# Top-k attention and two MLPs on one core: the first batch's values loaded once, and another drawn order of all instructions

## The chip, the cores and the metric

The program runs on one core of a Trainium2 chip, as one launch. The metric is the device time of a run in microseconds, taken as the median of several runs. The core's engines are TensorE (PE, with its weight loads as PEld), VectorE (DVE), ScalarE (ACT), GpSimd (POOL) and SyncE (SP); here SP issues every DMA, and its queue is served in order.

## The reference

For 4 batches of 8 heads, 576 positions and 64 channels:

```python
scores = scale * np.matmul(q, k.transpose(0, 1, 3, 2))
kth = np.partition(scores, -32, axis=-1)[..., -32:-31]
scores = np.where(scores >= kth, scores, -1e9)
attn = softmax(scores)                # max subtracted, sum + 1e-9
x = np.matmul(attn, v)                # -> 2304 tokens x 512
x = softplus(x @ w_in1) @ w_out1      # 512 -> 2048 -> 512
h = x @ w_in2
x = (h - tanh(h)) @ w_out2
```

All arrays are float32. The kernel keeps each operand as a sum of two float16 numbers (hi and lo), scaled by a power of two, and forms three products of every matrix product.

## The kernel before, in words

**Work.** The 576 queries of a batch are four tiles of 128 and a rest of 64. A chunk is two tiles of one batch (256 tokens); the rests of two batches form a chunk of their own. A visit (`visit_load`, L1205) is one pair of heads of one chunk; there are 32. It loads keys, queries and values of the pair, and the second visit to a pair takes the prepared keys and values back from a copy in DRAM. Per tile of a visit: scores on PE (`front`), copied to SBUF by ACT, four MAX8 and three MATCH_REPLACE8 on DVE to find the 32nd largest, an exponential on ACT, the hi and lo halves on ACT and POOL, a DMA transpose (pT), the product with the values on PE (`back`, L1400), and at the end of a visit a transpose into the chunk's x (tiles xy).

**Weights.** Each of the four weight matrices comes in 8 groups of 1 MB (`weight_load`, L867). A group is cast on ACT, combined on DVE, squared and summed on PE for its scale (`weight_convert`, L918), and split into whi and wlo (`weight_split`, L962): whi on ACT for all four; wlo on POOL for the first and the fourth, on PE and ACT for the second, on DVE for the third. While a tile is not yet needed, its room serves as staging: parts of whi and wlo of the later matrices hold raw weights or constants.

**MLP.** Once a chunk's x is complete, each layer runs in 8 steps: `gemm1` (24 matmuls into h), an activation on ACT (and DVE and POOL), `gemm2` into y. Layer 1 of a chunk needs all of the first two matrices; layer 2 the last two.

**Scales of the values.** Before the values of a batch can be split (`visit_prep_v`, L1302: one ACT and one DVE instruction of 128x640 per pair), a power-of-two scale is needed. `v_norm` (L1039) loads all values of the batch a second time, as five pieces of 128x460 into free xy tiles, squares each on ACT with a running sum, and forms the scale `sx` on DVE and PE. For batch 0 that is called where the loop over tiles stands at n == VN, which is 0. The pair's own values come by three DMAs in `visit_load`, into a single buffer v (NVR = 1), so that the next pair's load waits for the split of the one ahead.

**Order.** All operations are first recorded (`Recorder`), each with a rank from its place in the program. `order` (L557) lays them out with a list scheduler (`place`) that has a cost for every instruction: the ranks get random noise from SEED, the schedule is refined over TURNS rounds, and the best is taken. Then each entry of SHIFTS moves the ranks again: one with a number draws noise of a given size for the operations of some engines in a time window, one with names (V: values, P: preparation of a visit, N: norms, L and W: load and conversion of weights, M: MLP, S: tiles) adds a constant. The result is a fixed order on every engine. `idle` (L594) puts filler matmuls, whose result nobody reads, into longer gaps that the plan foresees on PE (L664).

Already in the file stands `first_v_load` (L1189), which with V0 = 1 takes the place of `v_norm(0)` and of the value loads of batch 0's visits; with V0 = 0 it isn't called.

Of the kernel before, what the change touches and what calls it, by code (L numbers as in the profile page):

```python
# [44 lines left out]
V0 = 0  # L45
# [33 lines left out]
SEED = 1322  # L79
# [12 lines left out]
VN = 0  # L92
# [7 lines left out]
NH = 2  # L100
NPX = 2
# [21 lines left out]
QLM = 0  # L123
SPC = 640.0

SHIFTS = (
# [12 lines left out]
    (22991, 679021, 687021, 2500, "PDAGS"), ("M0", 220737, 520737, -300, "PDAG"), (72979, 149882, 157882, 200, "PDAGS"),  # L139
# [3 lines left out]
    (86590, 883276, 903276, 2500, "SA"), (94052, 867481, 875481, 1000, "PDAGS"), (39752, 741704, 801704, 200, "PDAGS"),  # L143
# [10 lines left out]
    (63116, 1018776, 1168776, 1000, "PDAGS"), ("N2", 277145, 317145, -3000, "PDAGS"), (79700, 731025, 751025, 200, "PDAGS"),  # L154
# [7 lines left out]
    (275, 843642, 863642, 2500, "PDAGS"), (54408, 328307, 336307, 200, "PDAGS"), ("P", 183450, 191450, -10000, "PDAGS"),  # L162
# [9 lines left out]
    ("S,P,V", 81321, 101321, -1000, "PDAG"), (32745, 441991, 741991, 100, "S"), (6720, 146714, 166714, 400, "PDAGS"),  # L172
# [498 lines left out]
def topk_attention_two_mlps(  # L671
# [64 lines left out]
    def spare(early=None):  # L736
# [3 lines left out]
        if not early:  # L740
            return al("px", NPX, [P, 512], F32, pb)
# [831 lines left out]
    def new_acc(T):  # L1573
        return [al("y", 2, [P, 512], F32, pb) for _ in range(T // P)]
# [353 lines left out]
```

## Time and profile before

| | |
|---|---|
| median of 3 runs | 1112.79 us (1110.7 to 1116.18) |
| the profiled execution: time, span | 1111.59 us, 1109.9 us |
| granted TensorE clock, mean | 0.977 |
| busy over the span: PE, DVE, ACT, POOL | 998.6, 928.0, 898.2, 769.7 us |
| weight loads on PE (PEld) | 785.7 us |
| data moved by DMA | 152.06 MB, of it 73.01 MB read from HBM |
| PE in the chain that ended last | 58% (DVE 15%, ACT 10%, POOL 7%) |

The table is one execution on the chip. Busy shares over the whole span hide that the stages differ: in forty equal slices of the span PE stands at 2 to 7 tenths in the first six and at 9 or more nearly everywhere after; DVE stands at 9 or 10 tenths from the second to the thirty-third slice and near zero at the end; the DMA engines are full in the first five. So the stages are read one at a time.

### The profile page before, as it was taken

How to read it: one execution, taken by the hardware profiler on the slowest of the kernel's cores; microseconds unless marked ns; L12 is line 12 of the kernel's file. 1: busy time of each engine (PE TensorE's matmuls, PEld its weight loads, DVE VectorE, ACT ScalarE, POOL GpSimd, SP SyncE). 2: the span in 40 equal slices, each digit the busy share in tenths (PEclk: the TensorE clock that was granted, in tenths of full speed). 3: DMA queues.
4: the chain of work that ended last, by engine and by line, in shares of the span. 5: the costliest groups of instructions: out<-in, count | busy, mean ns of one | idle time of the engine just before them, and what ended most of it. 6: DMA issues, size and time to landing. Idle time of an engine off the chain costs nothing.

```text
span 1109.9 us, 27484 instructions
## 1 busy us (share of the span) xinstructions
PE 998.6 (90%) x9996; PEld 785.7 (71%) x9996; DVE 928.0 (84%) x2059; ACT 898.2 (81%) x1825; POOL 769.7 (69%) x1136
## 2 busy tenths in 40 slices
PE   2446749989889999999999999999999999999998
PEld 1323437867578767876899778876787689967965
DVE  3999999989999999799999999999999999310111
ACT  6999999989899988788999898988888777643422
POOL 6795438998888666568987675787957667443423
PEclk9999868999999999999999999999999999999999
DMA  9999996538777856437877565566755462300000
GB/s 289 279 284 273 292 283 182 150 91 184 138 166 190 213 95 132 69 71 150 187 156 168 114 144 108 76 139 130 148 108 101 88 126 46 49 6 20 2 10 20
DMA packets 317496, 152.06 MB, mean 137 GB/s; under 512 B 264624, under 2 KB 308656, under 8 KB 317360
## 3 DMA queue, kind: packets, MB, share of 16 engines
q1 hardware_dynamic: 317360, 150.30, 60.3%
q8 instruction: 78, 1.28, 0.5%
q14 instruction: 58, 0.48, 0.1%
HBM read 73.01 MB, written 15.37 MB: 80 GB/s over the span
## 4 chain that ended last, share of the span: by engine, by line
PE 58%; DVE 15%; ACT 10%; POOL 7%; issue 5%; DMA 4%; SPq 0%; ACTq 0%; POOLq 0%; DVEq 0%
PE h L667 26%; PE y L667 24%; DVE m L667 6%; DVE x L667 5%; PE px L667 4%; PE s L667 4%; ACT ssb L667 2%; ACT x L667 2%; POOL hl L667 2%; POOL wlo L667 1%; ACT wlo L667 1%; ACT whi L667 1%; DMA pT<-hl 1%; ACT hl L667 1%; ACT r L667 1%
## 5 line engine op out<-in xcount | busy, mean ns | idle before, releaser
L667 PEld LDWEIGHTS <-whi 128*128 128x128 f16 (+1 forms) x3994 | 373.1, 99 | 85.7 <-DVE whi L667 25.7
L667 PE MATMUL h<-xy,whi 128*128 128x256 f16 (+1 forms) x2560 | 395.3, 262 | 2.2 <-DVE xy L667 1.9
L667 PE MATMUL h<-xy,wlo 128*128 128x256 f16 (+1 forms) x1280 | 324.7, 262 | 0.0
L667 DVE MAX8 m<-x 128x8 f32<-128x576 f32 x432 | 313.7, 745 | 0.7
L667 POOL TENSOR_TENSOR hl<-x,hl 128x512 f16<-128x512 f32 (+1 forms) x288 | 217.3, 771 | 77.5 <-ACT hl L667 63.5
L667 PEld LDWEIGHTS <-wlo 128*128 128x128 f16 (+1 forms) x1986 | 195.4, 99 | 39.1 <-DVE wlo L667 11.8
L667 DVE MATCH_REPLACE8 x<-m,x 128x576 f32<-128x576 f32 x288 | 212.7, 740 | 0.0
L667 PE MATMUL y<-g,whi 128*128 128x256 f16 (+1 forms) x1280 | 200.5, 263 | 1.2 <-POOL g L667 1.2
L667 PE MATMUL y<-whi,g 128*128 128x512 f16 x576 | 194.4, 379 | 3.0 <-POOL g L667 3.0
L667 POOL TENSOR_TENSOR g<-r,g 128x512 f16<-128x512 f32 (+1 forms) x160 | 171.9, 1076 | 15.9 <-PE y L667 8.4
L667 PE MATMUL y<-g,wlo 128*128 128x256 f16 (+1 forms) x640 | 163.1, 263 | 0.0
L667 DVE SCALAR_TENSOR_TENSOR r<-h,hinb,r 128x512 f32<-128x512 f32 (+1 forms) x80 | 54.9, 688 | 116.7 <-ACT r L667 116.4
L667 PEld LDWEIGHTS <-g 128*128 128x128 f16 x864 | 81.2, 98 | 75.9 <-POOL g L667 3.9
L667 ACT ACTIVATE x<-ssb,nb,tiny 128x576 f32<-128x576 f32 x136 | 117.6, 866 | 10.2 <-DVE m L667 5.5
L667 PE MATMUL s<-kT,qT 128*128 128x288 f16 x512 | 91.2, 304 | 29.2 <-ACT ssb L667 14.9
L667 DVE MAX8 m<-ssb 128x8 f32<-128x576 f32 x144 | 107.3, 745 | 10.7 <-ACT ssb L667 10.0
L667 PEld LDWEIGHTS <-pT 128*128 128x128 f16 (+1 forms) x2240 | 89.7, 102 | 32.1 <-issue 16.5
L667 PE MATMUL y<-wlo,g 128*128 128x512 f16 x288 | 109.1, 379 | 0.0
L667 DVE MATCH_REPLACE8 x<-m,ssb 128x576 f32<-128x576 f32 x144 | 106.5, 739 | 0.0
L667 PE MATMUL px<-vhl,pT 128*128 128x65 f16 (+1 forms) x2240 | 96.1, 196 | 8.9 <-DMA pT<-hl 5.3
L667 POOL TENSOR_SCALAR r<-r,gsb 128x512 f32<-128x512 f32 (+1 forms) x80 | 52.6, 658 | 66.3 <-ACT g L667 65.8
L667 ACT CAST hl<-x 128x576 f16<-128x576 f32 x144 | 96.1, 670 | 0.5
(153 smaller groups left out, 1616.2 us busy)
## 6 DMA issues: line engine op xcount, KB each, us to landing
whi<-in_moe_w_in_dram SPq DMA_DIRECT2D x11, 1023.0 KB, 7.5
whi<-in_moe_w_out_dram SPq DMA_DIRECT2D x7, 1023.5 KB, 6.4
vd<-vhl SPq DMA_DIRECT2D x16, 330.0 KB, 4.3
vhl<-vd SPq DMA_DIRECT2D x16, 330.0 KB, 3.4
kd<-kT SPq DMA_DIRECT2D x32, 160.0 KB, 2.8
kT<-kd SPq DMA_DIRECT2D x32, 160.0 KB, 2.7
xy<-in_moe_w_out_dram SPq DMA_DIRECT2D x18, 255.8 KB, 3.0
qraw<-in_q_dram SPq DMA_DIRECT2D x32, 128.0 KB, 3.4
```

What stands on the lines that cost most here:

```text
L667: fn(*a, **k)
```

## The change

Four things. V0 = 1 and VN = 1: for batch 0 the values are loaded once by `first_v_load`, four pairs with three DMAs each, at the next loop position; pair 0 into the buffer v, pairs 1 to 3 into a part of wlo of the third matrix that is not yet written; four ACT squares of 128x640 give the scale. The place of pairs 1 to 3 in that tile is turned round, so that pair 3 lies highest. A new SEED and a new list of SHIFTS draw another order of everything. And three lines about PSUM buffers (NYB, pw, y3) are added, whose conditions need NPX == 1; NPX is 2 here.

```diff
-V0 = 0
+V0 = 1
-SEED = 1322
+SEED = 1962
-VN = 0
+VN = 1
+NYB = 2
...
 SHIFTS = (
-    (14983, 315778, 335778, 1000, "A"), (37653, 130389, 150389, 6000, "G"),
...
+    (86327, 773281, 1073281, 100, "G"), ("N2", 206017, 2000000, 1000, "PDAGS"),
...
         if not early:
-            return al("px", NPX, [P, 512], F32, pb)
+            one = NPX == 1 and "y3" not in slots
+            return al("pw" if one else "px", 1 if one else NPX, [P, 512], F32, pb)
         turn_[0] += 1
-        return al("hy"[turn_[0] % 2], 2, [P, 512], F32, pb)
+        return al("hy"[turn_[0] % 2], (NH, NYB)[turn_[0] % 2], [P, 512], F32, pb)
...
-                c = (NG - 1) * GW - 2 * 2 * (NB + 1) * D * p
+                c = (NG - 1) * GW - 2 * 2 * (NB + 1) * D * (NP - p)
...
     def new_acc(T):
-        return [al("y", 2, [P, 512], F32, pb) for _ in range(T // P)]
+        if NPX == 1 and wdone[0] == 4 * NG and "y3" not in slots:
+            slots["y3"] = [0, slots["y"][1] + slots["pw"][1]]
+        tag, n = ("y3", 3) if "y3" in slots else ("y", 2)
+        return [al(tag, n, [P, 512], F32, pb) for _ in range(T // P)]
```

`first_v_load`, which was in the file and is now called:

```python
def first_v_load():
    ss = al("vss", 2, [P, NP], F32, cap=5)
    for p in range(NP):
        dst = first_v[p]
        nc.sync.dma_start(dst[:, :, 0:NB, :], v[0, 2*p : 2*p+2, 0 : NB*P, :]...)
        for r in (slice(0, SL), slice(SL, P)):
            nc.sync.dma_start(dst[r, :, NB, :], v[0, 2*p : 2*p+2, NB*P : S, :]...)
        j, st = xy_take([P, 2 * (NB + 1) * D], F16, "vst")
        xy_free.append(j)
        nc.scalar.activation(st, dst..., AF.Square, accum_out=ss[:, p : p + 1])
    tot = tiny()
    nc.vector.tensor_reduce(tot, ss, axis=AX.X, op=ALU.add)
    pow2_scale(col_norm(tot, 1), sx[0], ix[0])
```

## Rows read from the trace of the kernel before

**Rows 1.** Stages of the span: busy PE, PEld, DVE, ACT, POOL; clock, DMA, GB/s

```profile
0.00:172.00 172.00, 86.91 (x621) 56.49 (x622) 152.43 (x351) 156.70 (x315) 105.70 (x144) 0.88 1.05 280
172.00:260.00 88.00, 80.14 (x790) 68.03 (x789) 82.62 (x191) 82.64 (x183) 85.13 (x131) 0.96 0.58 147
260.00:480.00 220.00, 209.80 (x2109) 165.36 (x2107) 211.93 (x475) 195.34 (x409) 163.12 (x245) 0.99 0.69 146
480.00:960.00 480.00, 476.05 (x5211) 386.56 (x5209) 463.30 (x1009) 412.68 (x837) 360.83 (x547) 1.00 0.59 119
960.00:1110.00 150.00, 145.72 (x1279) 109.28 (x1275) 17.76 (x36) 50.84 (x84) 54.92 (x70) 1.00 0.05 13
```

**Rows 2.** The same view for the filler matmuls alone (L664): PE, PEld

```profile
172.00:260.00 88.00, 9.65 (x76) 7.27 (x76) 0.96 0.58 147
260.00:480.00 220.00, 4.94 (x25) 2.61 (x25) 0.99 0.69 146
480.00:960.00 480.00, 1.17 (x9) 0.89 (x9) 1.00 0.59 119
```

**Rows 3.** Timeline: last transpose into the first chunk's x, first matmul of the MLP

```profile
168.16 1.20 SPq L667 DMA_TRANSPOSE xy<-xs  x1
172.24 0.63 PE L667 MATMUL h<-xy,whi 128*128 128x256 f16 x2
```

**Rows 4.** ACT before 172 us, grouped: busy, mean ns of one | idle before

```profile
L667 ACT CAST wlo<-whi 128x1024 f16<-128x1024 bf16 x17 | 22.9, 1345 | 6.2 <-DMA whi<-in_moe_w_in_dram 6.2
L667 ACT ACTIVATE whi<-whi,tiny 128x1024 f16<-128x1024 f32 x17 | 21.0, 1236 | 1.1 <-DVE tiny L667 1.0
...
L667 ACT ACTIVATE xy<-xy 128x460 f32<-128x460 f32 x12 | 7.0, 592 | 0.0
...
L667 ACT CAST wlo<-wlo 128x1024 f16<-128x1024 bf16 x5 | 6.7, 1341 | 0.0
L667 ACT CAST wlo<-xy 128x256 f16<-128x256 bf16 x15 | 6.4, 501 | 0.0
...
L667 ACT ACTIVATE vhl<-v,tiny 128x640 f16<-128x640 f32 x4 | 3.3, 833 | 0.0
L667 ACT ACTIVATION_READ_ACCUMULATOR xy<-xy 128x1 f32 x15 | 3.0, 201 | 0.0
```

**Rows 5.** DMA engines before 172 us: packets, data, rate

```profile
DMA packets 59555, 48.09 MB, mean 280 GB/s; under 512 B 39316, under 2 KB 56724, under 8 KB 59540
```

**Rows 6.** SP's queue in order of time: issues of batch 0's values

```profile
6.15 3.00 SPq L667 DMA_DIRECT2D v<-in_v_dram  x2
...
17.33 1.69 SPq L667 DMA_DIRECT2D xy<-in_v_dram  x3
...
26.80 0.56 SPq L667 DMA_DIRECT2D xy<-in_v_dram  x1
...
48.45 0.52 SPq L667 DMA_DIRECT2D v<-in_v_dram  x1
...
93.44 1.46 SPq L667 DMA_DIRECT2D v<-in_v_dram  x2
```

**Rows 7.** The chain that ended last, two pieces of the opening: start, us

```profile
58.73 0.62 SPq L667
...
62.86 4.94 DMA kraw<-in_k_dram
```

**Rows 8.** Timeline: the scale of batch 0's values, and its first use

```profile
35.64 0.19 DVE L667 TENSOR_SCALAR tiny<-n 128x1 int32<-128x1 int32 x2
...
43.80 0.83 ACT L667 ACTIVATE vhl<-v,tiny 128x640 f16<-128x640 f32 x1
```

**Rows 9.** DVE before 172 us, grouped: one form of the top-k

```profile
L667 DVE MAX8 m<-x 128x8 f32<-128x576 f32 x57 | 41.9, 747 | 0.1
```

**Rows 10.** Timeline of DVE: batch 0's last values split, third matrix's first wlo

```profile
109.90 0.87 DVE L667 SCALAR_TENSOR_TENSOR vhl<-v,tiny,vhl 128x640 f16<-128x640 f32 x1
...
128.82 0.47 DVE L667 SCALAR_TENSOR_TENSOR wlo<-xy,tiny,whi 128x256 f16<-128x256 f32 x1
```

More of the change, by code (lines that the diff above doesn't have):

```diff
@@ L123 @@
 QLM = 0
+NYB = 2
 SPC = 640.0
 SHIFTS = (
[12 rows of a table removed]
-    (22991, 679021, 687021, 2500, "PDAGS"), ("M0", 220737, 520737, -300, "PDAG"), (72979, 149882, 157882, 200, "PDAGS"),
[3 rows of a table removed]
-    (86590, 883276, 903276, 2500, "SA"), (94052, 867481, 875481, 1000, "PDAGS"), (39752, 741704, 801704, 200, "PDAGS"),
[10 rows of a table removed]
-    (63116, 1018776, 1168776, 1000, "PDAGS"), ("N2", 277145, 317145, -3000, "PDAGS"), (79700, 731025, 751025, 200, "PDAGS"),
[7 rows of a table removed]
-    (275, 843642, 863642, 2500, "PDAGS"), (54408, 328307, 336307, 200, "PDAGS"), ("P", 183450, 191450, -10000, "PDAGS"),
[9 rows of a table removed]
-    ("S,P,V", 81321, 101321, -1000, "PDAG"), (32745, 441991, 741991, 100, "S"), (6720, 146714, 166714, 400, "PDAGS"),
[13 rows of a table removed]
[6 rows of a table added]
+    (45861, 315750, 355750, 100, "PDAGS"), (74532, 672388, 732388, 100, "D"), (40357, 597981, 657981, 100, "PDAGS"),
[9 rows of a table added]
+    (85308, 310569, 350569, 100, "PDAGS"), (41834, 1002330, 1022330, 6000, "PDAGS"), (86243, 727558, 787558, 400, "SA"),
[6 rows of a table added]
+    (18309, 200830, 220830, 200, "PDAGS"), (2026, 977709, 1277709, 6000, "PDAGS"), ("W2", 207490, 357490, 20000, "PDAGS"),
[17 rows of a table added]
+    (2993, 1004414, 1024414, 2500, "PDAGS"), (36391, 313315, 373315, 100, "D"), (50062, 298444, 306444, 1000, "PDAGS"),
[7 rows of a table added]
+    (88304, 209604, 217604, 400, "PDAGS"), (4748, 161365, 181365, 100, "PDAGS"), (39302, 102789, 122789, 2500, "PD"),
[8 rows of a table added]
+    (24339, 973107, 1013107, 6000, "PDAGS"), (4225, 572153, 632153, 2500, "S"), (46791, 593738, 613738, 200, "PDAGS"),
+    (36113, 682980, 702980, 1000, "A"), (89711, 528204, 536204, 400, "A"), (7941, 510941, 530941, 200, "A"), (55060, 744424, 764424, 6000, "S"),
+    (62163, 329902, 349902, 2500, "G"), (65759, 811680, 819680, 6000, "P"), (53464, 551140, 571140, 1000, "D"), (81936, 827662, 847662, 200, "PDAGS"),
+    (28563, 833653, 873653, 100, "PDAGS"), (44601, 753307, 761307, 1000, "A"), (93312, 882130, 890130, 400, "PDAGS"),
+    (10851, 816201, 1116201, 100, "PDAGS"), (35963, 847784, 855784, 2500, "G"), (86908, 814315, 874315, 400, "PDAGS"),
+    (75628, 671644, 691644, 400, "SA"), (44943, 777816, 785816, 2500, "PDAGS"), (13754, 182796, 202796, 100, "PDAGS"),
[6 rows of a table added]
 )
```

113 rows, old and new, of the table SHIFTS are left out of this document.

## The prediction

> **What bounds the kernel now.** I read the stages of the span first [rows 1]. From 480 us on PE is busy 476.1 of 480 us and 145.7 of 150: nothing that the change touches is short there. Before 480 us it is not so. Until 172 us PE is busy 86.9 us, while ACT is busy 156.7 and DVE 152.4 of 172 (from about 20 us on they have hardly a gap), and the DMA engines stand at a share of 1.05. From 172 to 480 us PE is busy 289.9 of 308 us, but 14.6 of that are fillers whose result nobody reads [rows 2], so useful PE work is 275.3 of 308, 89%; DVE, with 294.6 of 308, paces it. Next the timeline where the MLP begins [rows 3]: the last transpose into the first chunk's x is issued at 168.2, and the first matmul into h runs at 172.2. All later PE work is fixed by the problem, so the time is the start of the MLP, plus that work, plus the gaps behind the start. The gaps are 26.3 us idle (7.9, 10.2, 4.0 and 4.3 in the last four stages, 0.1 of it past the span's end) and 15.8 us of fillers, 42 us together. A change can win in two places: an earlier start, which ACT and DVE set, or smaller gaps before 480 us.
>
> **The change part by part.**
>
> *The three lines on PSUM buffers* ask for NPX == 1, and NPX and NH are 2: the same buffers are handed out as before. Nothing.
>
> *The squares for the scale.* Five ACT squares of 128x460 with their accumulator reads go: 5 x (0.592 + 0.201) = 3.97 us [rows 4]. Four of 128x640 come. The trace has no square of that size; the ACT instruction of that shape on the same values takes 0.833, so 4 x (0.833 + 0.201) = 4.14. Below, the 460-wide price would make it 3.2, above, scaling 0.592 by 640/460 gives 4.1. I take +0.2 us on ACT, which has no cover before 172 us.
>
> *The loads.* Five DMAs of 230 KB go (1.15 MB); the twelve loads by pair stay the same in number and bytes, and move to one block at the next loop position. Two costs hang on this. The DMA engines move 48.09 MB in the opening at 280 GB/s [rows 5], so 1.15 MB are 4.1 us of theirs; that is the gain if they set the pace, and nothing if they don't. And SP's queue loses the five norm issues of 17.3 to 26.8 us; nine value issues stood between 48.5 and 94.9 us, 6.4 us of queue time over seven rows of which the first and the last are shown [rows 6]. These stand in front of the transposes pT, kT and qT and of the key loads, on which the tiles of chunk 0 hang. What the chain shows of that is less: one value issue of 0.62 us lies on it, a few issues ahead of a key load of 4.94 us [rows 7]. So from 0.6 (the chain) to 6.4 us (all nine) can be won there if the block in front is hidden, and up to 7.4 us lost (twelve issues at 0.62) if it is not. I take -3.2 us, half of the nine issues, since the queue is loaded and the chain passes through it, but only once with a value issue on it.
>
> *The scale, one tile later.* The scale is written at 35.8 us and first used at 43.8 [rows 8], 8.0 us of slack. Moving the call by one tile is one tile of top-k, 7 x 0.747 = 5.2 us [rows 9], less than the slack. Nothing; without the cover 5.2 us.
>
> *The parking place.* Pairs 1 to 3 lie in wlo of the third matrix until their split. In the order of before the last split begins at 109.9 and ends at 110.8 us, and DVE first writes the third matrix's wlo at 128.8 [rows 10]: 18 us of cover, and pairs 1 to 3 start only in the fourth group. Nothing; if the new order drew weight groups forward by more than that, the DVE write would wait, and behind it on DVE the top-k of chunk 0. In return the single buffer v no longer makes each pair's load wait for the split ahead; no such wait of length is on the chain, so I give it nothing.
>
> *The order.* Here the trace of before has no row, only bounds. A weight group costs ACT 1.345 + 1.236 = 2.58 us [rows 4]. Before 172 us ACT casts 17 + 5 + 15/4 = 25.75 groups. The first layer of chunk 0 needs 16; 9.75 stand ahead of it that it doesn't need, and 6.25 of all 32 stand behind. Pushing all 9.75 back would start the MLP 25.2 us sooner; pulling all 6.25 ahead would start it 16.1 us later. I take the middle of the two ends, -4.5 us, something under two groups. That the sign is negative is the weakest step here.
>
> *The sum.* +0.2 - 3.2 - 4.5 = -7.5 us at the start of the MLP. Not all of it reaches the end: until 480 us PE does useful work for only 89% of the time because DVE and the others feed it, so of a sooner start that share gets through, -6.7 us; what is late next is the x of the second and third chunk, which waits for top-k on DVE. The profiled execution took 1111.6 us (span 1109.9 and 1.7 around it): 1104.9. The median of the runs is 1.2 above the profiled one, so 1106 for the median.
>
> **The rivals.** About 0.5%, 5.6 us, is what a measurement of this kernel can tell from no change.
>
> *The transfers were hidden anyway* (1112.8). The opening is paced by ACT and DVE, whose work the change doesn't lessen (+0.2 us), and the order is worth nothing on the chip. For it: ACT's and DVE's busy time in the opening, and that a single long DMA wait after the first microseconds is on the chain [rows 1, 7]. Against it: SP's part in the chain. 1112.8 + 0.2 = 1113. Beside the DMA share of 1.05 stands a rule of the Trainium skill (Perfetto Trace Analysis, Identifying the Most-Contended Engine): occupancy of the sixteen DMA engines misleads, and use of HBM should be read in its place. The page DMA: Bandwidth & Descriptors, Specifications, puts the HBM limit of a core at some 358 GB/s; the 280 GB/s of the trace lie under it, so by that rule the engines are not the bound, which is this rival. Whether it holds here no row before the change shows.
>
> *The block of loads stands in the way* (1120). All twelve value issues are placed together on SP in the first 40 us, ahead of the first transposes. Its price is twelve issues at 0.62, 7.4 us, plus 0.2 on ACT: 1112.8 + 7.6 = 1120.4. It decides from the point where the first pT leaves SP more than 5.6 us later than now, or the first matmul into h comes after 178 us. For it: SP serves in order, and two of pair 0's issues already took 3.0 us [rows 6]. Against it: SP is less filled from 20 to 40 us than from 40 to 100, and a planner lays the block out piece by piece.
>
> *The order closes gaps* (1099). A third of the 42 us of idle time and fillers behind the start goes: -14. 1112.8 - 14 = 1099. For it: 7.9 us idle and 9.7 of fillers lie in the 88 us right behind the start [rows 1, 2], where POOL is busy 85.1 of 88, so the order of POOL's work decides there. Against it: nothing in the edit takes work from POOL.
>
> **How the numbers follow.** The forecast 40%, with its own range 1101 to 1111; hidden anyway 22%; the block in the way, or an order that pulls weights ahead, 22%; closed gaps 16%. Faster by over 0.5% (under 1107.2): 0.30 of the forecast's 0.40, 0.01 of the hidden case, all 0.16 of the closed gaps, 0.47. Slower by over 0.5% (over 1118.4): 0.20 of the third case, 0.02 of the hidden one, 0.22. The rest, 0.31, is within. The range runs from 1094 (closed gaps together with an earlier start, some 19 us) to 1121 (the third case's price); beyond it lie about 0.05 below and 0.10 above, where the order's upper bound of 16 us belongs.
>
> **What would show it.** Right: the five loads into xy from the values are gone; the first matmul into h lies at 164 to 168 us; fewer than 25 groups are cast before it; value issues are gone from SP between 48 and 95 us; idle time plus fillers behind the start stay near 42 us. The hidden case: start at 170 to 174 and gaps unchanged. The third case: start after 178, pT late. The closed gaps: start as now, but under 30 us of idle time and fillers. Wrong altogether would be a gain or a loss behind 480 us, where I count nothing, or a DVE write of the third matrix's wlo that waits for a split of values.

## The result, and the profile after

The kernel after takes 1119.4 us (median of 12 runs, 1116.7 to 1122.7), the kernel before, beside it on the same chips, 1112.0 (12 runs): a ratio of 1.0063, 95% interval 1.0046 to 1.0080. I forecast 1106. The sign was wrong, and the time lies near the upper end of the range. The profiled execution has a span of 1115.9 us and a granted clock of 0.963 of full speed on average, where before it was 0.977. The lower clock doesn't show in PE's work: without fillers PE is busy for 980.4 us in all, before for 982.9.

The stages of the span after, as in [rows 1]:

```profile
0.00:172.00 172.00, 86.90 (x628) 56.64 (x629) 149.52 (x344) 155.03 (x309) 102.85 (x142) 0.80 1.01 266
172.00:260.00 88.00, 72.08 (x680) 60.10 (x679) 84.31 (x179) 77.40 (x170) 79.50 (x122) 0.93 0.58 146
260.00:480.00 220.00, 213.76 (x2181) 168.87 (x2179) 215.18 (x488) 198.06 (x421) 166.96 (x256) 1.00 0.71 150
480.00:960.00 480.00, 474.69 (x5179) 384.68 (x5177) 462.83 (x1013) 409.69 (x836) 355.85 (x543) 1.00 0.60 119
960.00:1116.00 156.00, 151.73 (x1352) 114.86 (x1349) 18.83 (x39) 54.47 (x92) 59.32 (x77) 1.00 0.07 16
```

The fillers alone, as in [rows 2] (their line is L676 now), PE and PEld:

```profile
172.00:260.00 88.00, 11.80 (x70) 7.73 (x70) 0.93 0.58 146
260.00:480.00 220.00, 6.26 (x50) 4.67 (x50) 1.00 0.71 150
480.00:960.00 480.00, 0.68 (x4) 0.19 (x2) 1.00 0.60 119
```

The timeline at the MLP's start, as in [rows 3]:

```profile
168.44 1.22 SPq L679 DMA_TRANSPOSE xy<-xs  x1
...
170.00 0.59 PE L679 MATMUL h<-xy,whi 128*128 128x256 f16 x2
```

The three views give the balance. The MLP starts at 170.0 us, 2.2 sooner than in [rows 3]. Behind 172 us PE is idle for 15.9, 6.2, 5.3 and 4.2 us (each stage less its busy time; the last without 0.1 past the span's end), and fillers take 18.7: together 50.4 us, where [rows 1, 2] gave 42.0. So 2.2 us are won at the start and 8.4 lost behind it; that is 6.2, and the spans differ by 6.0. The loss has one place: idle time and fillers from 172 to 260 us are 27.7 us against 17.5 before (+10.2), and the stage after that gives 2.6 back (12.5 against 15.1).

ACT before 172 us, grouped as in [rows 4]:

```profile
L679 ACT CAST wlo<-whi 128x1024 f16<-128x1024 bf16 x17 | 22.9, 1349 | 4.4 <-DMA whi<-in_moe_w_in_dram 3.6 <-DMA whi<-in_moe_w_out_dram 0.8
...
L679 ACT CAST wlo<-wlo 128x1024 f16<-128x1024 bf16 x5 | 6.8, 1350 | 0.6 <-DMA wlo<-in_moe_w_out_dram 0.4 <-DMA wlo<-in_moe_w_in_dram 0.3
...
L679 ACT CAST wlo<-xy 128x256 f16<-128x256 bf16 x12 | 5.6, 490 | 0.1
...
L679 ACT ACTIVATE xy<-wlo 128x640 f16<-128x640 f32 x3 | 2.2, 726 | 0.3 <-DMA wlo<-in_v_dram 0.3
```

That is 17 + 5 + 12/4 = 25 weight groups cast, where it was 25.75, and the new squares.

Inside the stage from 172 to 260 us one window stands out. From 230 to 240 us, after and then before (columns as above):

```profile
230.00:240.00 10.00, 4.41 (x30) 2.94 (x29) 10.00 (x17) 3.02 (x7) 6.66 (x11) 0.77 0.01 2
```

```profile
230.00:240.00 10.00, 9.88 (x94) 8.04 (x94) 8.92 (x21) 9.03 (x19) 10.00 (x16) 0.84 0.36 90
```

After, PE is busy for 4.4 of the ten us and ACT for 3.0, and the DMA engines hardly at all; DVE is busy all the time, but with 17 instructions instead of 21. DVE's timeline there, and POOL's:

```profile
225.66 0.74 DVE L679 MAX8 m<-ssb 128x8 f32<-128x576 f32 x1
226.32 0.62 DVE L679 SCALAR_TENSOR_TENSOR wlo<-wlo 128x256 int32<-128x256 int32 x1
226.87 5.97 DVE L679 TENSOR_SCALAR tiny<-tiny 128x8 int32<-128x8 int32 x1
226.94 0.08 DVE L679 MATCH_VALUE_LOAD x<-m,x 128x8 f32 x1
227.01 6.47 DVE L679 MATCH_REPLACE8 x<-m,x 128x576 f32<-128x576 f32 x1
```

```profile
226.60 0.68 POOL L679 MEMSET whi<- 128x256 f16 x1
227.10 1.16 POOL L679 TENSOR_TENSOR g<-r,g 128x512 f16<-128x512 f32 x1
228.19 0.67 POOL L679 MEMSET xy<- 128x256 f16 x1
228.70 0.69 POOL L679 TENSOR_SCALAR r<-r,gsa 128x512 f32<-128x512 f32 x1
...
232.49 0.31 POOL L679 TENSOR_TENSOR hl<-x,hl 128x64 f16<-128x64 f32 x1
232.90 0.27 POOL L679 TENSOR_SCALAR nb<-m,tiny 128x1 f32<-128x1 f32 x1
```

An instruction on 8 numbers a partition lasts 5.97 us; alone it takes 0.15 (a measurement below). It ends at 232.84, in the first gap of POOL's row since 225.1 (232.80 to 232.90). Behind it a MATCH_REPLACE8 of 0.74 shows 6.47. What PE waits for then are weight groups that DVE combines after the wait:

```profile
234.74 0.41 PE L679 MATMUL px<-whi 128*128 128x128 bf16 x2 [3.76 <-DVE whi L679]
...
237.18 0.64 PE L679 MATMUL px<-xy 128*128 128x128 bf16 x4 [1.80 <-DVE xy L679]
```

The chain that ended last passes through this place; its piece "DVE x" at 227.02 (x is the copy of the scores on which the top-k works) is the wait and the MATCH_REPLACE8 behind it:

```profile
217.09 2.91 DVE x L679
227.02 6.46 DVE x L679
```

### The profile page after: what moved, and what is told of

Same layout as the page of the kernel before. It is cut to its first block, busy times and chain, and to the rows that moved or that the text cites. A ratio compares the mean times of both kernels' runs of the same rounds, so it can differ in the third digit from the quotient of the medians.

```text
span 1115.9 us, 27515 instructions
## 1 busy us (share of the span) xinstructions
PE 999.2 (90%) x10008; PEld 785.2 (70%) x10008; DVE 930.7 (83%) x2059; ACT 894.7 (80%) x1823; POOL 764.5 (69%) x1136
## 4 chain that ended last, share of the span: by engine, by line
PE 58%; DVE 13%; ACT 9%; POOL 7%; DMA 6%; issue 5%; SPq 1%; POOLq 0%; ACTq 0%; DVEq 0%
PE h L679 25%; PE y L679 25%; DVE x L679 5%; DVE m L679 5%; PE px L679 4%; PE s L679 3%; POOL hl L679 2%; ACT x L679 2%; ACT ssb L679 1%; SPq L679 1%; ACT wlo L679 1%; ACT r L679 1%; DVE wlo L679 1%; POOL wlo L679 1%; POOL g L679 1%
## 5 line engine op out<-in xcount | busy, mean ns | idle before, releaser
L679 DVE MATCH_REPLACE8 x<-m,x 128x576 f32<-128x576 f32 x288 | 218.6, 760 | 0.0
L679 POOL TENSOR_TENSOR g<-r,g 128x512 f16<-128x512 f32 (+1 forms) x160 | 171.9, 1075 | 17.8 <-PE y L679 10.2
```

The source lines that it names most:

```text
L679: fn(*a, **k)
```

## The experiments

The theories that were named before the runs: A, DVE instructions wait while POOL runs without a pause; B, the value loads at the front delay the opening; C, the new order as a whole shares the engines worse. D to H came with the later runs, and E is not the same theory throughout: in the first two measurements apart from the kernel it says that a memset on POOL lets DVE in, in the third that memsets hold it. Every ratio is to runs of the kernel before on the same chip; it is taken over all runs and can differ from the quotient of two medians by 0.1%. In the table, "first h" is the first matmul into h, where the MLP starts; the times and gaps are of the profiled execution.

| kernel | first h, us | idle and fillers 172 to 260, us | the same behind 172, us | ratio, 95% interval |
|---|---|---|---|---|
| before | 172.2 | 17.5 | 42.0 | 1 |
| after | 170.0 | 27.7 | 50.4 | 1.0063 [1.0046, 1.0080] |
| loads alone | 173.3 | 18.5 | 44.0 | 1.0006 [0.9989, 1.0023] |
| order alone | 175.3 | 23.4 | 50.1 | 1.0119 [1.0090, 1.0148] |
| loads twice, order of before | 172.0 | 18.6 | 43.8 | 1.0008 [0.9993, 1.0023] |
| after, one read | 169.3 | 25.2 | 45.7 | 1.0026 [1.0009, 1.0042] |
| after, two reads | 170.0 | 23.1 | 46.5 | 1.0015 [0.9997, 1.0032] |
| after, no memsets in the row | 169.3 | 25.4 | 50.0 | 1.0016 [0.9997, 1.0035] |
| before, four reads | 172.6 | 18.2 | 38.7 | 0.9972 [0.9957, 0.9987] |

**The two parts apart.** The loads alone: the order of before on every engine, the new loads and squares in the places of the old ones.

```diff
-V0 = 0
+V0 = 1        # VN stays 0; every engine's order as before, written out
...
```

> The value loads of batch 0 alone, in the order of before: every engine runs its instructions in the order of the kernel before, the five norm loads and squares are replaced by the loads of pairs 1 to 3 and four squares in the same places, and the nine later value loads are gone. Theory A: about as before, 1110 to 1114, for the long stalls of DVE lie where they lay. Theory B: slower by 3 to 6 us, 1115 to 1118. Theory C: as before, 1110 to 1114. The prediction's term for the loads would give 1109.

Measured 1114.3 us, ratio 1.0006. The order alone: the order of after, with the old norm and the old loads by pair.

```diff
-V0 = 1
+V0 = 0        # VN = 1; every engine's order as after, written out
...
```

> The new order alone, with the old value loads: five norm loads and squares in the places of the block, the loads of pairs 1 to 3 each behind the split of the pair ahead (batch 1's first value load moves behind them, since it uses the same buffer). Theory A: the stalls come with the order, 1116 to 1121, if the stall at 227 us is still there. Theory B: the front is free again, 1112 to 1115. Theory C: 1118 to 1121.

Measured 1126.4 us, ratio 1.0119. In the order of before the loads bring nothing that these runs can tell, and the new order carries the loss. It is even slower without the early loads: the first h comes at 175.3 us, and the wait is there, 5.97 us at 231.9. (To keep the order, the first value load of the next pair and one part of a split had to come later than in after; so the 7 us between order alone and after are not a clean price of the loads.)

**The wait at 227 us.** POOL reads one column of the waiting instruction's result first, so that it pauses there until DVE is done.

```diff
 for o in done:
+    for d in GATES.get(o.i, ()):        # {1241: (790,)}: before POOL's g<-r,g at 227.1 us
+        out = self.ops[d].calls[0][1][0]
...
+        out = out[:, 0:1]
...
+        self.real.gpsimd.tensor_scalar(self.scr, out, 1.0, 1.0, op0=ALU.mult, op1=ALU.mult)
```

> The changed kernel with one more instruction on POOL: before its g<-r,g at 227.1 us it reads one column of the 128x8 result that DVE forms at 226.9 us (5.97 us long there, where the other 128x8 forms take 0.15), so that POOL pauses until DVE has it. Theory A (the loss is DVE instructions that cannot run while POOL works without a pause): the instruction takes under 0.5 us, the 5.8 us go, 1119.4 - 5.8 = 1113.6. Theory B (the value loads at the front delay the opening, and the stall at 227 is covered): unchanged, 1118 to 1121. Theory C (the new order shares the work out worse): unchanged, 1118 to 1121.

Measured 1115.3 us, ratio 1.0026: 4 of the 7 us come back, where theory A gave 5.8. DVE's instruction takes 0.43:

```profile
226.46 0.43 DVE L690 TENSOR_SCALAR tiny<-tiny 128x8 int32<-128x8 int32 x1
226.54 0.08 DVE L690 MATCH_VALUE_LOAD x<-m,x 128x8 f32 x1
226.61 0.94 DVE L690 MATCH_REPLACE8 x<-m,x 128x576 f32<-128x576 f32 x1
```

But at 252.7 us a TENSOR_TENSOR of 128x8 now takes 2.43 us, which took 0.21 in after. With the same read at the waits of 39.1 and 217.0 us too:

> The changed kernel with three such reads on POOL, at 39.1, 217.0 and 226.9 us, where DVE instructions ran 2.0, 2.1 and 5.8 us over their usual time. Theory A: up to 9.9 us go, less some 0.5 us of POOL for each read: 1110 to 1112. Theory B and theory C: 1117 to 1121.

Measured 1115.9 us, ratio 1.0024 [1.0006, 1.0043]. The two further reads gave nothing: the early waits were gone, but the first h came at 171.1 us, no sooner. The wait at 217 lies on the chain above too, with 2.91 us, and its end gave nothing that can be told: a place on the chain is not yet a price.

**The opening.** All engines' orders as in after, but on SP the first three weight blocks are issued 1st, 8th and 9th, by the trace, instead of 5th, 12th and 18th.

> The changed kernel, all engines' orders as they are, but on SP the first three weight blocks are issued 1st, 9th and 10th of the first eighteen loads instead of 5th, 12th and 18th, and values behind them. Theory B (the value loads at the front delay the opening, and that delay stays to the end): the first cast starts at 8.5 to 9 us instead of 11.25 and the time is 1117, 2 to 2.5 us less. Theory A or C (the opening is bound by the sum of all loads, whatever their order): 1119 to 1120.

Measured 1123.8 us, ratio 1.0095 [1.0073, 1.0117]: 4 us worse, with the first h at 175.5. The first cast starts at 9.3 us instead of 11.25 and wins nothing: what ACT runs next, a square of values, waits 5.30 us for its load and starts at 15.9 us instead of 12.8, and the split of keys behind it at 17.7 instead of 14.6. Theory B in this form falls, and so does the idea that the order of the loads doesn't matter. With the reads at 227 and 252.7 us on top:

> The changed kernel with the weights issued first, the read at 227 us that gave back 4 us, and a second one at the place to which the wait went then (252.7 us, 2.2 us too long). Theories A and B together: 1119.4 - 4.1 - 2 - 1.6 = 1111.7, ratio 0.998 to 1.000. A alone: 1113.7. Neither: 1115.3, what the first read alone gave.

Measured 1120.8 us, ratio 1.0069 [1.0051, 1.0087]: the two reads are worth 3 us here, and the weights first stay a loss.

**What holds DVE.** Three measurements apart from the kernel: POOL runs a row, DVE arrives beside it. First with rows of one form, each POOL instruction waiting for the one before:

> A measurement of the disputed cost by itself; it computes none of the reference. Forty small stretches: after a common start POOL runs nothing, six subtractions, six scalings or six memsets of 128x512 without a pause, or two subtractions, a wait for ACT and four more; beside it DVE runs one kind of instruction twice, between MAX8s. Theory A (a DVE instruction of two SBUF inputs, or a tensor_scalar, can't start its work until POOL really pauses, and a memset on POOL holds it like any other): beside six POOL instructions of 0.5 to 1.2 us each, a tensor_scalar of 128x8 int32, 0.14 us alone, lasts until the row of POOL ends, 2 to 6 us; the scalar_tensor_tensor of 128x576 too; MAX8, and what the 'pause' row shows, ends at the pause after about 2 us. Rival D (the two engines only share a bandwidth): every DVE instruction is at most twice its time alone, 0.3 us for the small one, and the pause makes no difference. Rival E (only POOL's arithmetic holds it, a memset doesn't, as the kernel's own plan assumes): long beside subtractions and scalings, 0.14 us beside memsets.

Neither A nor D. The small tensor_scalar took 0.78 us beside subtractions, the tensor_tensor of 128x1 0.77, both until the running subtraction ended, not the row. Beside memsets they took 0.27 and 0.14. MAX8, MATCH_REPLACE8, reciprocal, reduce and a float tensor_scalar of 128x1 were never held. E, that a memset lets DVE in, came nearest. Then without dependences inside the row:

> The first measurement beside POOL again, with a result tile of its own for every POOL instruction; it computes none of the reference. There each POOL instruction waited for the one before (0.05 to 0.09 us between them), and DVE came in at the first such gap: 0.65 us instead of 0.14 beside subtractions, 0.14 beside memsets. Here POOL's instructions overlap, as in the kernel's row from 225.1 to 232.8 us. Theory A (DVE comes in only when POOL stands still; two instructions that overlap leave no such moment, and a memset among them neither): tensor_scalar of 128x8 and tensor_tensor of 128x1 take 3 to 6 us beside seven subtractions and beside the mixed row of subtraction, memset and scaling, and about 2 us where the row pauses; MAX8 0.74 throughout. Rival E (a memset lets DVE in): about 0.5 to 1.2 us in the mixed row, until its first memset, and 0.14 beside memsets alone. Rival D (shared bandwidth): under 0.8 us everywhere.

Beside seven memsets the int32 tensor_scalar was held to the end of the row:

```profile
17.02 0.76 DVE L43 MAX8 m<-z 128x8 f32<-128x576 f32 x1 [5.84 <-ACT z L42]
17.69 2.92 DVE L64 TENSOR_SCALAR ti<-ti 128x8 int32<-128x8 int32 x1
17.75 2.87 DVE L79 MAX8 m<-z 128x8 f32<-128x576 f32 x1
```

Beside subtractions it took 0.78, in the mixed row 1.24, and the tensor_tensor of 128x1 beside memsets 0.14. So here a POOL instruction that reads holds both for its own length, and memsets in a row hold the int32 tensor_scalar, alone of the five forms tried, for the row. That is against A (3 to 6 us beside subtractions), against D (under 0.8 everywhere) and against E (0.14 beside memsets). Then the rows of the traces, form by form:

> POOL's row of 225.1 to 232.8 us of the changed kernel, the same without its memsets, and its row of 284.0 to 291.0 us of the kernel before, form by form, beside four kinds of DVE instruction that arrive 0.7 to 1.7 us after the row's start; it computes none of the reference. Theory A (held until the row ends): the int32 tensor_scalar lasts 4 to 7 us in the first row whatever its moment, the scalar_tensor_tensor of 128x1 2 to 6 us in the third. Rival G (held for one POOL instruction, or for memsets that follow each other, as the two measurements before showed): at most 1.3 us each; then what made 6 us lies in something that these rows leave out (semaphores, traffic of DMA and the other engines). Rival E (the memsets do it): long in the first row, at most 1.3 us in the bare one and the third.

DVE beside the row of 225 to 233 us (here the row runs from 31.6 to 39.6), and behind the dots beside the same row without memsets:

```profile
31.59 0.76 DVE L58 MAX8 m<-z 128x8 f32<-128x576 f32 x1 [7.76 <-ACT z L57]
32.26 0.34 DVE L89 RECIPROCAL red<-red 128x1 f32<-128x1 f32 x2
32.52 3.14 DVE L92 TENSOR_SCALAR ti<-ti 128x8 int32<-128x8 int32 x1
32.58 3.08 DVE L106 MAX8 m<-z 128x8 f32<-128x576 f32 x1
35.70 3.90 DVE L92 TENSOR_SCALAR ti<-ti 128x8 int32<-128x8 int32 x1
...
65.72 0.62 DVE L92 TENSOR_SCALAR ti<-ti 128x8 int32<-128x8 int32 x1
66.25 0.75 DVE L106 MAX8 m<-z 128x8 f32<-128x576 f32 x1
66.92 0.52 DVE L92 TENSOR_SCALAR ti<-ti 128x8 int32<-128x8 int32 x1
```

With memsets it is held up to 3.90 us, without them 1.14 at most, in the row of 284 to 291 us 0.53 at most; the scalar_tensor_tensor of 128x1 never over 1.13. In this measurement it is the memsets (E as it stands here), and of the four forms tried the tensor_scalar alone; G's bound of 1.3 us falls. It isn't always held to the row's end: the 3.14 us end at 35.66, where a memset ends and a scaling is already running. The test in the kernel turns the six memsets of that row into scalings, in the same places:

```diff
 for fn, a, k in o.calls:
+    if o.i in SCALED:                   # the six memsets of 225.5 to 232.0 us
+        zero = self.unit1.to_broadcast(list(a[0].shape))
+        self.real.gpsimd.tensor_scalar(a[0], zero, 0.0, 1.0, op0=ALU.mult, op1=ALU.mult)
+        continue
     fn(*a, **k)
```

> The changed kernel with the six memsets in POOL's row of 225.1 to 232.8 us written as scalings of a column by zero (about 0.5 us each, in the same places of the row, which stays without a pause); nothing else. Theory E (the int32 tensor_scalar is held by memsets in POOL's row): its 5.97 us at 227 us fall to at most 1.5 and the time to that of the run with one read, 1115 to 1116, ratio 1.002 to 1.004. Rival H (any row of POOL without a pause holds it): 5 to 6 us still, 1118 to 1120, ratio 1.005 to 1.007.

Measured 1115.7 us, ratio 1.0016 [0.9997, 1.0035]. POOL still runs without a pause there, and DVE gets in at 227.58, behind the scaling that it met and the product after it (226.41 to 227.57):

```profile
225.64 0.95 POOL L685 TENSOR_SCALAR whi<-unit 128x256 f16<-128x256 f32 x1
226.41 1.16 POOL L687 TENSOR_TENSOR g<-r,g 128x512 f16<-128x512 f32 x1
227.53 0.77 POOL L685 TENSOR_SCALAR xy<-unit 128x256 f16<-128x256 f32 x1
```

```profile
225.88 1.70 DVE L687 TENSOR_SCALAR tiny<-tiny 128x8 int32<-128x8 int32 x1
...
226.32 1.92 DVE L687 MATCH_REPLACE8 x<-m,x 128x576 f32<-128x576 f32 x1
228.16 0.43 DVE L687 SCALAR_TENSOR_TENSOR whi<-whi 128x256 int32<-128x256 int32 x1
```

5.97 us became 1.70, a little over the 1.5 that E allowed, and the time fell as with the read. H, which gave 5 to 6 us, is out. (The profiled execution of this run took 1118.7 us, 3 us above the median; its gaps in the table belong to that execution.)

Not every wait in the kernels has a memset beside it, though. DVE and POOL of after at 217 us:

```profile
217.01 2.98 DVE L679 SCALAR_TENSOR_TENSOR x<-ssb,m,x 128x576 f32<-128x576 f32 x1
```

```profile
216.96 0.68 POOL L679 TENSOR_TENSOR wlo<-wlo,whi 128x256 f16<-128x256 f32 x1
217.59 1.16 POOL L679 TENSOR_TENSOR hl<-x,hl 128x512 f16<-128x512 f32 x1
218.70 0.67 POOL L679 TENSOR_TENSOR wlo<-whi 128x256 f16<-128x256 f32 x1
```

The DVE instruction, 0.80 us elsewhere, outlasts three POOL instructions in a row that all read. The waits at 39.1 us in after, at 288.0 and 506.6 in before and at 252.7 with one read are of this kind, beside three to five such instructions without a memset. No measurement apart from the kernel shows this: there the forms of 128x1 with two inputs never took over 1.13 us.

**The loads again, doubled.** The kernel before issues the five loads of 1.18 MB a second time, into idle tiles.

```diff
     fn(*a, **k)
+    if o.i in TWICE:                    # five places on SP between 17 and 36 us
+        j, name = TWICE[o.i]
+        fn, a, k = self.ops[j].calls[0]
+        fn(self.homes[name][:, 0 : a[0].shape[-1]], a[1], **k)
```

> The kernel before with the five loads of the first batch's values for its column norm (1.18 MB) issued a second time, between 17 and 36 us, into tiles that are idle until 178 us: the cost that the change takes away, doubled. The prediction's step (opening bound by SP's issues and DMA, 3.2 us for these loads; 4.1 us by bytes at 280 GB/s): 1112.3 + 3 to 4 = 1115.5 to 1116.5, ratio 1.003 to 1.004. Theory F (the opening is bound by the preparation of weights on ACT and DVE, busy 91% and 89% of it, and the loads are beside it): 1112 to 1113, ratio 0.999 to 1.001, and the first MLP matmul stays at 172 to 173 us.

Measured 1113.2 us, ratio 1.0008, first h at 172.0. The DMA engines simply moved more: 287 GB/s before 172 us instead of 280 [rows 5], and 339 instead of 290 from 17 to 36 us. The opening doesn't wait for these loads. The time is the one that theory F gave; that weights on ACT and DVE bound the opening, as F has it, the run doesn't show.

**The same waits in the kernel before.** Reads at its two longest waits, 288.0 and 506.6 us:

> The kernel before, with one POOL read of one column of DVE's result put into POOL's row at the two places where a DVE instruction waited longest (288.0 us: 2.8 us too long; 506.6 us: 2.5 us too long), so that POOL pauses there. Theory A (such waits carry to the end, some 70% of them, as the first such read gave back 4 of 5.75 us): 1112.3 - 0.7 x 5.3 = 1108.6, ratio 0.996 to 0.998. Rival C (the order's own sharing of the engines sets the time, a wait is made up for): 1112 to 1113, ratio 0.999 to 1.001.

Measured 1111.2 us, ratio 0.9986 [0.9969, 1.0002]: not told from no change. A wait of 1.56 us came up at 250.0. With that one and 723.9 us as well:

> The kernel before with four reads: the two at 288.0 and 506.6 us, and two where the wait went or stayed then (249.97 us, 1.3 us too long, and 723.9 us, 1.4 us too long). Theory A: 1111.2 - 0.7 x 2.7 = 1109.3, ratio 0.996 to 0.998. Rival (each read only moves the wait to the next row of POOL that has no pause): 1111 to 1112, ratio 0.998 to 1.000.

Measured 1109.1 us, ratio 0.9972 [0.9957, 0.9987], faster than both kernels. Three of the waits went; the one at 723.9 stayed (1.69 us, now at 720.2); the idle time and fillers behind 172 us fall from 42.0 to 38.7. In after, with reads at 227 and 252.7 us:

> The changed kernel with two reads: at 227.1 us, and at 252.7 us where the wait went then (2.2 us too long). Theory A (the rest of the loss is such waits too): 1115.3 - 0.7 x 2.2 = 1113.7, ratio 1.000 to 1.002. Theory C (the rest is the order: work put off until after the MLP's start): 1115 to 1116, ratio 1.002 to 1.004.

Measured 1114.7 us, ratio 1.0015 [0.9997, 1.0032], no longer told from before, and not decided between A and C. The wait at 252.7 is gone; 2.97 us at 217 remain.

## Why the prediction was wrong

*What bounds the kernel.* Right where it matters for the sum: the time is the MLP's start, the work behind it and the gaps. The balance above closes with these three. The rival of the closed gaps said too that POOL's order decides from 172 to 260 us. But the sum had no term for those gaps; it let 89% of an earlier start through and held the rest fixed. They grew from 42.0 to 50.4 us, by 8.4.

*The squares.* Priced at +0.2 us. Three squares of 128x640 took 0.726 each, where I put 0.833; four with their reads of 0.186 would be 3.65 us against 3.97 taken away, -0.3. Right in being nothing.

*The loads, -3.2.* Wrong: in the order of before no gain can be told, by the loads alone (1.0006, from 0.9989 up, where 89% of 3.2 us would be 0.9974) and by the loads doubled (1.0008). In the new order no run prices them cleanly. The half of nine issues had no row behind it; the chain's 0.6 was the better bound. Seven of the nine did leave the stretch from 48 to 95 us, as forecast, and nothing came of it. The rule that the Trainium skill gives in Perfetto Trace Analysis, Identifying the Most-Contended Engine (a high share of the DMA engines misleads) held here: at a share of 1.05 there was room for 1.18 MB more.

*The scale, and the parking place.* Right. Read as in [rows 8, 10], the scale is written by 25.8 us and first used at 27.4, without a wait, though the cover is 1.6 us instead of 8.0; the last split of values begins at 105.7, and DVE first writes the third matrix's wlo at 129.6.

*The order, -4.5.* The step that failed, and the one I had called the weakest. I took the order to be worth what it does to the MLP's start, in weight groups. Before 172 us 25 groups are cast instead of 25.75, and the start moved by 2.2 us, where the sum had 7.5. The gaps, to which the sum gave no term, took back 8.4. What I left out is that an order decides which instruction of DVE stands beside which of POOL. At 227 us one int32 tensor_scalar met a row with six memsets and held DVE for 5.97 us, and behind it PE for weights (3.76 and 1.80 us). Ending that wait gave back 4 of the 7 us, in two ways that have only this in common. The wait that took its place gave back about half a us more (1115.3 and 1114.7, inside the runs' spread). The rest of the loss has no shown cause: with one read the stage from 172 to 260 us still holds 25.2 us of idle time and fillers, where before held 17.5.

*The rivals.* The loads were hidden anyway, as the first rival said, but the order was not worth nothing. The second had about the right time, 1120, by another mechanism: the first h came sooner, not after 178 us. The third saw the right place (POOL's order in the 88 us behind the start) and the wrong sign. A rival was missing: gaps that open. Of the signs that I named, the start at 170.0 us fits the hidden case, 25 groups are not fewer than 25, and the gaps fit none.

*What stays open.* After two reads after stands 0.15% above before, its interval reaching to none. But before with four reads is 0.43% below after with two (0.9972 against 1.0015), so the new order shows no gain, though it starts the MLP 2 us sooner; like for like this is not, since 2.97 us at 217 stay in after. It does less ahead of the start, and DVE is busy 215.2 us from 260 to 480 instead of 211.9; whether that put-off work eats the gain was argued from the windows and not tried. Open too is what holds DVE over several POOL instructions that read: the scalar_tensor_tensor at 288.0 us in before takes 3.02 us, and the same form beside the same row took 0.52 at most apart from the kernel. Nor did the row with memsets hold the tensor_scalar longer than 3.90 us apart from it, where the kernel shows 5.97. And the read that ends a wait shifts all that follows, so part of each gain may be luck.

## What to carry to other kernels

An order that a planner draws can be judged by its start only if the gaps behind it are looked at as well: subtract busy time and fillers from each stage, and see where the difference of two kernels lies before any theory. A tiny vector instruction that lasts microseconds is a wait for another engine; read what that other engine runs at the time, by kind of instruction. And a share of the DMA engines over 1 is no proof that loads bind: adding a load a second time settles it for that load in one run.

## What the hardware showed

A tensor_scalar of 128x8 int32, 0.15 us alone, took 0.78 us beside subtractions on POOL, 2.92 beside seven memsets, up to 3.90 in a row where memsets stand between other instructions, 5.97 in the kernel, and 1.70 there with scalings in the memsets' places. A tensor_tensor of 128x1 took 0.77 beside subtractions and 0.14 beside memsets. The Trainium skill (SBUF — State Buffer, Who interferes with whom) says that a DVE instruction with two SBUF inputs contends with a GpSimd instruction that reads SBUF and not with one that only writes, and that one in a 2-port mode contends with GpSimd, where whichever issues first blocks the other for its whole instruction. The first half agrees with 0.77 and 0.14. The second agrees beside subtractions (0.78), but beside memsets the wait went on over several instructions (2.92 to 5.97); there the measurement decides. The wait of 2.98 us at 217.0, of a form with two inputs beside three instructions that read, goes over several too. That the int32 tensor_scalar runs in a 2-port mode no run here shows.
